# A cross network on one Trainium2 core: TensorE's warm-up cut into 41 products of 128 columns

## The chip, the core and the metric

The kernel runs on one core of one Trainium2 chip. A core has a matrix engine (TensorE; the profile writes PE for its products and PEld for its weight loads), three engines for elementwise work (VectorE or DVE, ScalarE or ACT, GpSimd or POOL), a queue engine (SyncE or SP), and 16 transfer engines that carry all DMA traffic. The working memory has 128 partitions; TensorE writes its results to a second memory, PSUM, of eight banks of 512 fp32 columns per partition. Every engine works through its own list of instructions in order and waits on semaphores that other engines or finished transfers raise.

The metric is device time in microseconds (us), from the first to the last thing that the program does on the chip. It is given as the median of several runs of the same program.

## The reference

The computation is the cross network of a recommender model, "DCN v2", over 4096 rows of 416 features with six layers, in bf16:

```python
B, F, D, L = 4096, 26, 16, 6
Din = min(F * D, 1024)          # 416
x0 = normal(B, Din) * 0.05
ws = normal(L, Din, Din) * 0.05
bs = normal(L, Din) * 0.05

def reference(x0, ws, bs):
    x = x0
    for l in range(ws.shape[0]):
        x = x0 * (x @ ws[l] + bs[l]) + x
    return x
```

Each layer is a product of the current 4096 x 416 matrix with a 416 x 416 matrix, a bias, an elementwise product with the first input, and a sum.

## The kernel before

**Tiling.** The features are the contraction of each layer, so the kernel keeps the activations transposed: features on the partitions, rows of the batch along the free dimension. 416 features are three full blocks of 128 (`XM`, written 0 to 2 as `m` or `k`) and a rest of 32 (`XR`). The batch is cut into two halves `s` of 2048 rows, and each half into four groups `g` of 512 columns. The rests of four groups are stacked on the 128 partitions of `XR`, so that one elementwise instruction handles four groups of 32.

**Inputs.** `x0` comes in twice. Its first 384 features are brought in by eight transposing transfers (`load_x0t`, line 77, all on SP's queue), each for one group of 512 rows, straight into `XM[0]`. The last 32 features (`xrem`) come as they lie in memory, with 64-byte segments (`load_xrem`, line 82): for the first half of the batch in two transfers of 64 partitions each on ScalarE's queue (lines 111 and 314), for the second half in one on SP's queue (line 123). They are turned on VectorE, 32 x 32 at a time (`x0_rem`, lines 160 to 167): a transpose (line 164), copies into `XR[0]` (line 165, one on ScalarE and one on VectorE), and a swapped copy `XRx` (line 167). The first of these two transfers is issued by ScalarE behind its copy of `bsb` (the biases) at line 110, and so after the biases are there; the second is issued behind ScalarE's copy of the first half of `XR`, and so after the first one has landed and been turned. Weights come over ScalarE's queue for layer 0 and over SP's for the others.

**Order of work.** The program runs under a manual schedule: the order of the instructions in the source is the order on each engine. TensorE's list is: the warm-up; layer 0 of the first half of the batch (`first_layer(0)`); layer 0 of the second half; layers 1 to 4 (`for l in range(1, LL)`), in which both halves and the three blocks `m` follow each other; and the last layer, which is computed with the batch rows on the partitions so that the result can be written without a transpose.

**The start of layer 0.** In `first_layer(0)` TensorE first makes six blocks of three untiled products each of 512 columns (line 252, 18 products: three blocks `m` for each of the first two groups), then six products with the 32 remaining features (line 260), for which `XR[0]`'s first 64 partitions must be ready. Then come 72 column-tiled products for the other two groups (line 252 again, four of them side by side in the array), 12 products for the rest of the output (`mm_rem`, line 227), and then six products of line 260 that need the second 64 partitions of `XR[0]`.

**The warm-up.** Before TensorE has any data it multiplies a constant tile `warm` (128 partitions x 512 columns of 0.5) by itself into PSUM bank 0; the result is never read, since the first real product into that bank starts a new sum. VectorE fills `warm` in two instructions, columns 0 to 127 first (line 87), then 128 to 511 (line 88). The function is `pe_filler(n, cols)` at line 151; each call makes n products with the same 128 x 128 weights and cols moving columns. Lines 155 to 157 call it.

**Instructions.** Each product in the source is two instructions on TensorE, a weight load and the product itself. The loops are unrolled in Python, so that the whole program is one straight list for each engine; the transfers of kind "instruction" in the profile bring these lists in.

Of the kernel before, what the change touches and what calls it, by code (L numbers as in the profile page):

```python
# [16 lines left out]
def kernel(  # L17
# [10 lines left out]
    P = 128  # L28
# [5 lines left out]
    CW = 512  # L34
# [116 lines left out]
    def pe_filler(n, cols):  # L151
        for i in range(n):
            nc.tensor.matmul(PS[:, 0, 0:cols], lhsT=warm[:, 0:P], rhs=warm[:, 0:cols], start=True, stop=True, skip_group_check=True)  # L153

    pe_filler(3, P)
    pe_filler(9, CW)
    pe_filler(1, 2 * P)


    def x0_rem(s, p0, p1, parts):  # L160
# [346 lines left out]
```

## Time and profile before

| | |
|---|---|
| time, median of three runs | 129.51 us (129.34 to 129.51) |
| the profiled execution's own time | 130.67 us |
| its span, first to last instruction | 128.9 us |
| TensorE busy | 122.7 us, 1839 products |
| VectorE busy | 104.9 us |
| ScalarE busy | 85.9 us |
| GpSimd busy | 7.8 us |
| warm-up (line 153) | 13 products, 1.04 to 5.65 us |
| first real product (line 252) | 5.79 us |

How to read the profile: all times count from the start of the span. A row of the timeline has the start in us, the duration in us, the engine, the source line, the operation, what it writes `<-` what it reads, the shape, and `x` the number of instructions that were merged into the row; in brackets stands how long the engine had been idle before it and what ended that. A row of the chain has start, duration, engine or transfer, tile and line; the chain is followed back from the last instruction through whatever released each step. "issue" is time in which an engine waited for nothing that the profile shows. A row of the windows view has a stretch of the span, its length, the busy time of each engine asked for with the number of instructions in it, the granted TensorE clock (1.00 is full), the mean busy share of the 16 transfer engines and GB/s. A row of the transfer view has either a queue (q1 is SP's, q10 ScalarE's, q8 and q14 instruction lists) with its packets, megabytes and the time of its packets as a share of 16 engines over the window, or an issue with its count, size and median time from issue to landing.

[...]

### The profile page before, as it was taken

What the parts mean: (1) busy time and instruction counts of PE and PEld (TensorE: products, weight loads), DVE (VectorE), ACT (ScalarE), POOL (GpSimd) and SP (SyncE); (2) the same over time, 40 slices, a digit from 0 to 9 for tenths busy, and PEclk for the clock granted to TensorE, in tenths of its full rate; (3) what the DMA queues carried; (4) which work ended last, traced back from release to release, by engine and by line L of the source; (5) the groups of instructions that cost most, each with busy time, mean ns of one, the idle gap of its engine ahead of it and who ended that gap; (6) DMA issues with size and microseconds to landing.
All of it is one profiled execution on the core that took longest, in us unless ns stands there. A gap on an engine that the chain in (4) does not pass through costs nothing.

```text
span 128.9 us, 4251 instructions
## 1 busy us (share of the span) xinstructions
PE 122.7 (95%) x1839; PEld 55.5 (43%) x1839; DVE 104.9 (81%) x192; ACT 85.9 (67%) x99; POOL 7.8 (6%) x27
## 2 busy tenths in 40 slices
PE   6999799999999999999999999999999999999960
PEld 3344344444444434444444444444444444554430
DVE  3347399649598989898989898989899999998991
ACT  2657194795875775975775975678486686766860
POOL 4270000120000000000000000000005000000000
PEclk9999999999999999999999999999999999999999
DMA  3999989999991000000000000000398999986463
GB/s 87 264 199 163 196 148 242 221 299 343 335 334 51 8 0 5 0 5 0 5 0 0 5 0 5 0 5 0 65 138 162 120 245 218 225 264 223 149 225 104
DMA packets 41935, 16.31 MB, mean 127 GB/s; under 512 B 30838, under 2 KB 41916, under 8 KB 41916
## 3 DMA queue, kind: packets, MB, share of 16 engines
q1 hardware_dynamic: 39344, 15.53, 54.7%
q10 hardware_dynamic: 2572, 0.51, 2.4%
q8 instruction: 14, 0.23, 0.8%
q14 instruction: 5, 0.04, 0.1%
HBM read 6.07 MB, written 3.41 MB: 74 GB/s over the span
## 4 chain that ended last, share of the span: by engine, by line
PE 79%; DMA 10%; DVE 6%; issue 1%; ACT 1%; POOL 0%; DVEq 0%; POOLq 0%
PE PS L208 49%; PE PS L348 9%; DMA xrem<-in_x_dram 7%; PE PS L252 6%; PE PS L214 5%; PE PS L227 5%; DMA bsb<-in_bs_dram 3%; PE PS L220 2%; DVE o L445 2%; DVE t L442 1%; PE PS L260 1%; PE PS L357 1%; DVE xrt L164 1%; DVE o L428 1%; DVE t L425 1%; PE PS L361 1%
## 5 line engine op out<-in xcount | busy, mean ns | idle before, releaser
L172 ACT ACTIVATE t<-PS,bM 128x1024 bf16<-128x1024 f32 x56 | 58.1, 1114 | 23.6 <-PE PS L214 22.8
L208 PE MATMUL PS<-XM,WM 128*32 128x512 bf16 x1152 | 65.2, 380 | 0.0
L208 PEld LDWEIGHTS <-WM 128*32 128x32 bf16 x1152 | 29.7, 97 | 33.8 <-issue 5.1
L182 DVE TENSOR_TENSOR t<-t,XM 128x1024 bf16<-128x1024 bf16 x48 | 33.2, 691 | 5.5 <-ACT t L172 5.4
L183 DVE TENSOR_TENSOR XM<-t,XM 128x1024 bf16<-128x1024 bf16 x48 | 33.5, 698 | 2.6
L348 PE MATMUL PS<-WM,XM 128*128 128x416 bf16 x96 | 17.9, 340 | 0.0
L252 PE MATMUL PS<-XM,WM 128*32 128x512 bf16 (+1 forms) x234 | 16.5, 381 | 0.1
L424 ACT CAST t<-PS 128x832 bf16<-128x832 f32 x12 | 10.1, 854 | 4.3 <-PE PS L348 2.9
L348 PEld LDWEIGHTS <-XM 128*128 128x128 bf16 x96 | 8.9, 98 | 8.6 <-issue 2.1
L252 PEld LDWEIGHTS <-WM 128*32 128x32 bf16 (+1 forms) x234 | 7.8, 97 | 8.4 <-issue 1.8
L227 PE MATMUL PS<-XM,WM 128*32 128x512 bf16 x120 | 8.2, 379 | 0.0
L214 PE MATMUL PS<-XR,WR 32*128 32x512 bf16 x96 | 7.5, 379 | 0.0
L428 DVE TENSOR_TENSOR o<-t,XLrows 128x832 bf16<-128x832 bf16 x12 | 7.0, 592 | 0.4
L425 DVE TENSOR_TENSOR t<-t,X0rows 128x832 bf16<-128x832 bf16 x12 | 7.0, 587 | 0.4 <-ACT t L424 0.4
L180 DVE TENSOR_TENSOR XM<-t,XM 128x1024 bf16<-128x1024 bf16 x7 | 4.9, 697 | 2.7 <-ACT t L172 2.7
L196 ACT ACTIVATE t<-PS,bR 128x512 bf16<-128x512 f32 x10 | 6.8, 695 | 0.0
L326 POOL COPY XLrows<-scrR 128x512 bf16<-128x512 bf16 x2 | 1.7, 894 | 70.8 <-DMA scrR<-XR 70.8
L153 PE MATMUL PS<-warm 128*128 128x512 bf16 (+2 forms) x13 | 4.6, 536 | 1.0 <-DVE warm L87 1.0
L164 DVE STREAM_TRANSPOSE xrt<-xrem 64x256 bf16<-64x256 bf16 (+1 forms) x5 | 2.2, 476 | 4.0 <-DMA xrem<-in_x_dram 4.0
L441 ACT CAST t<-PS 128x416 bf16<-128x416 f32 x8 | 4.0, 505 | 1.0 <-PE PS L348 0.8
L189 ACT ACTIVATE t<-PS,bM 128x512 bf16<-128x512 f32 x4 | 2.6, 685 | 3.0 <-PE PS L260 3.0
L227 PEld LDWEIGHTS <-WM 128*32 128x32 bf16 x120 | 3.2, 97 | 3.3
(47 smaller groups left out, 54.9 us busy)
## 6 DMA issues: line engine op xcount, KB each, us to landing
X0rows<-in_x_dram SPq DMA_DIRECT2D x8, 416.0 KB, 7.8
WM<-in_ws_dram SPq DMA_DIRECT2D x5, 312.0 KB, 5.2
out_dram<-o SPq DMA_DIRECT2D x3, 416.0 KB, 4.6
out_dram<-o SPq DMA_DIRECT2D x6, 208.0 KB, 2.1
out_dram<-o SPq DMA_DIRECT2D x8, 104.0 KB, 1.7
WR<-in_ws_dram SPq DMA_DIRECT2D x4, 104.0 KB, 4.9
WM<-in_ws_dram ACTq DMA_DIRECT2D x1, 312.0 KB, 3.4
XM<-in_x_dram SPq DMA_TRANSPOSE x8, 5.4
```

Source lines behind the costliest of these rows:

```text
L172: nc.scalar.activation(t[:], pt.rearrange("p a b -> p (a b)"), ACT.Identity, bias=bM[:, m, l:l + 1], scale=1.0)
L182: nc.vector.tensor_tensor(out=t, in0=t, in1=x0c, op=ALU.mult)
L183: nc.vector.tensor_tensor(out=nxt[:, m, c0:c0 + 2 * CW], in0=t, in1=cur[:, m, c0:c0 + 2 * CW], op=ALU.add)
L196: nc.scalar.activation(tr[:, 0:CW], pr, ACT.Identity, bias=bR[:, l:l + 1], scale=1.0)
L208: nc.tensor.matmul(pts[g // 2][32 * q:32 * q + 32, g % 2, :], lhsT=WM[:, l, k, 128 * m + 32 * q:128 * m + 32 * q + 32], rhs=cur[:, k, c0:c ...
L214: nc.tensor.matmul(pts[g // 2][:, g % 2, :], lhsT=WR[32 * g:32 * g + 32, l, 128 * m:128 * m + 128], rhs=curR[32 * g:32 * g + 32, CW * s:CW ...
L227: nc.tensor.matmul(pr[32 * g:32 * g + 32, :], lhsT=WM[:, l, k, NK * P:D], rhs=cur[:, k, c0:c0 + CW], start=(first and k == 0), stop=((not ...
L252: nc.tensor.matmul(pt[q0:q1, gl, :], lhsT=WM[:, 0, k, 128 * m + q0:128 * m + q1], rhs=cur[:, k, c0:c0 + CW], start=(first and k == 0), sto ...
L348: nc.tensor.matmul(py[g // 2][:, g % 2, 0:D], lhsT=xL[:, k, q_cols(q, g)], rhs=WM[:, LL, k, :], start=(first and k == 0), stop=((not first ...
L424: nc.scalar.copy(tv, py[h][:, :, 0:D])
L425: nc.vector.tensor_tensor(out=tv, in0=tv, in1=X0rows[:, b0:b0 + 5:4, :], op=ALU.mult)
L428: nc.vector.tensor_tensor(out=o, in0=tv, in1=XLrows[:, b0:b0 + 5:4, :], op=ALU.add)
```

## The change

The three calls of the warm-up become one. Before, it is three products of 128 columns, nine of 512 and one of 256; after, 41 of 128. The weights, the tile `warm`, the PSUM bank and everything before and behind stay as they are.

```diff
@@ -152,9 +152,7 @@
         for i in range(n):
             nc.tensor.matmul(PS[:, 0, 0:cols], lhsT=warm[:, 0:P], rhs=warm[:, 0:cols], start=True, stop=True, skip_group_check=True)
 
-    pe_filler(3, P)
-    pe_filler(9, CW)
-    pe_filler(1, 2 * P)
+    pe_filler(41, P)
 
 
     def x0_rem(s, p0, p1, parts):
```

P is 128 and CW is 512. With `pe_filler(41, P)` no product reads columns 128 to 511 of `warm`; VectorE's second fill (line 88) stays in the program. Lines behind the change have numbers smaller by two in the kernel after.

## The prediction

> **What bounds the kernel now.** I read the page's busy table first, then the chain of work that ended last in order of time between 4 and 17 us, then the timeline of TensorE for the same stretch.
>
> ```profile
> PE 122.7 (95%) x1839; PEld 55.5 (43%) x1839; DVE 104.9 (81%) x192; ACT 85.9 (67%) x99; POOL 7.8 (6%) x27
> ```
> ```profile
> 4.70 3.97 DMA xrem<-in_x_dram
> 9.16 5.58 DMA xrem<-in_x_dram
> 14.76 0.78 DVE xrt L164 x2
> 15.57 0.38 DVE XR L165
> 16.00 0.78 PE PS L260 x6
> ```
> ```profile
> 1.04 4.61 PE L153 MATMUL PS<-warm 128*128 128x128 bf16 x13 [1.04 <-DVE warm L87]
> 5.79 4.31 PE L252 MATMUL PS<-XM,WM 128*128 128x512 bf16 x18
> 10.03 0.60 PE L260 MATMUL PS<-XR,WR 32*128 32x512 bf16 x4
> 10.30 0.39 PE L260 MATMUL PS<-XRx,WR 32*128 32x512 bf16 x2
> 10.62 4.07 PE L252 MATMUL PS<-XM,WM 128*32 128x512 bf16 x72
> 14.51 0.82 PE L227 MATMUL PS<-XM,WM 128*32 128x512 bf16 x12
> 16.00 0.60 PE L260 MATMUL PS<-XR,WR 32*128 32x512 bf16 x4 [0.66 <-DVE XR L165]
> ```
>
> TensorE is busy 95% of the span, but up to 16.0 us it does not set the end. There the chain runs through transfers: the first half of `xrem`, then the second half (issued 9.16, landed 5.58 later at 14.74), VectorE's transpose and copy, and then the product of line 260. TensorE has run dry 0.66 us before that product, and the warm-up is on no piece of this chain. The list of TensorE's waits has, beside the start, one row:
>
> ```profile
> PE PS L260 <- DVE XR L165: 0.7, 1, 0.7
> ```
>
> After 16.0 us it waits for no engine and no transfer. So the end moves by what moves the product at 16.00 us, and 0.66 us of lateness on TensorE before it is free.
>
> **The change part by part.** Columns first: 3 x 128 + 9 x 512 + 256 = 5248 and 41 x 128 = 5248. The same number streams; 13 products become 41, each with its weight load, so TensorE gets 28 products and 28 loads more (56 instructions). No transfer, wait or other engine's instruction moves in the code.
>
> *Duration of the warm-up.* Weight loads on TensorE by time (start, duration):
>
> ```profile
> 1.12 0.26 PEld L153 LDWEIGHTS <-warm 128*128 128x128 bf16 x2
> 1.23 0.15 PEld L153 LDWEIGHTS <-warm 128*128 128x128 bf16 x1
> 4.81 0.15 PEld L153 LDWEIGHTS <-warm 128*128 128x128 bf16 x1 [0.28 <-issue]
> 5.23 0.42 PE L153 MATMUL PS<-warm 128*128 128x256 bf16 x1
> 5.79 0.10 PEld L252 LDWEIGHTS <-WM 128*128 128x128 bf16 x1 [0.41 <-issue]
> 6.17 0.15 PEld L252 LDWEIGHTS <-WM 128*128 128x128 bf16 x1 [0.28 <-issue]
> 6.48 3.12 PEld L252 LDWEIGHTS <-WM 128*128 128x128 bf16 x15 [0.16 <-issue]
> ```
>
> The last 512-column piece starts with the load at 4.81, 5.23 - 4.81 = 0.42 us before the next piece; the 128-column ones are at the start 1.23 - 1.12 = 0.11 us apart: the load of the next piece runs while this one streams, in both shapes. 41 pieces at 0.11 us start last at 1.04 + 40 x 0.11 = 5.4 us, against 5.23 us for the 256-column piece now, whose columns end half a 0.42 later, about 5.45 us; the new last piece's end 0.11 later, about 5.5 us. The first real product starts at 5.79 us either way, because its transposed block of `x0`, issued at 0.71 us, lands at 5.7:
>
> ```profile
> XM<-in_x_dram SPq DMA_TRANSPOSE x1, 5.0
> ```
>
> The cover is those 0.3 us, and behind them the 0.66 us. The 512-column pieces also waited for VectorE's second fill of `warm`; the new ones need the first fill alone, worth under 0.1 us, which nobody sees. Cost: 0. Without the cover it would be what the pitch exceeds 0.11 us by, times 41.
>
> *Pace of TensorE.* The granted clock reads 1.00 in every window quoted below (third column from the end), yet the starts above say otherwise: 0.4 us per 512 columns until about 6.2 us, then 3.12 us for 15 pieces (0.21 each). The pace doubles after some 5 us of products. The new warm-up streams the same columns over the same time, so I take the doubling as unmoved: 0. The ends: 0.2 us earlier per real product for the two slow ones (a gain that the wait at 16.0 us swallows), and the late opening priced under the rivals.
>
> *Instruction fetch: the moved step.* 56 more instructions ahead of everything else shift all later fetches of TensorE's instruction stream. The page's queue list, windows of the transfer view (one line each, windows 15.3 to 15.5, 22.5 to 22.7, 38.3 to 38.4, 49.9 to 50.0, 57.0 to 57.1 us; the share is of 16 engines over the window), and the products started by then:
>
> ```profile
> q8 instruction: 14, 0.23, 0.8%
> ```
> ```profile
> q8 instruction: 1, 0.02, 30.4%
> q8 instruction: 1, 0.02, 40.8%
> q8 instruction: 1, 0.02, 68.3%
> q8 instruction: 1, 0.02, 86.4%
> q8 instruction: 1, 0.02, 83.2%
> ```
> ```profile
> 0.00:15.40 15.40, 14.16 (x121) 1.00 1.04 188
> 0.00:22.60 22.60, 20.76 (x235) 1.00 1.00 186
> 0.00:38.40 38.40, 36.56 (x519) 1.00 1.05 236
> 0.00:49.90 49.90, 48.06 (x723) 1.00 0.82 187
> 0.00:57.00 57.00, 55.16 (x851) 1.00 0.72 164
> ```
>
> Each fetch is one packet of 0.23 MB / 14 = 16 KB; the one at 15.3 to 15.5 us took 0.304 x 16 x 0.2 = 0.97 us of one transfer engine. In the quiet stretch they come 851 - 723 = 128 products apart (with their loads 256 instructions), so they follow the count: 723 = 5 x 128 + 83, hence the first belongs to product 83. Product 83 is number 83 - 13 - 18 - 6 = 46 of the 72 that start at 10.62 us; four take 0.215 us (15 untiled ones 3.12 us; four tiled share a pass), so it starts at 10.62 + 46/4 x 0.215 = 13.1 us. The fetch came at 15.4, 2.3 us later, while transfers were busy; the second came 235 - 128 - 83 = 24 products late (1.3 us at 0.054), the fourth 519 - 3 x 128 - 83 = 52 (2.8 us). So under load the lag is 1.3 to 2.8 us. After the change the 83rd product is what is now the 55th, 18th of the 72: 10.62 + 18/4 x 0.215 = 11.6 us, and the fetch comes at 12.9 to 14.4 us instead of 15.4. What else moves then, in the same view for 11.5 to 13.77 us:
>
> ```profile
> q10 hardware_dynamic: 1040, 0.07, 40.2%
> ```
>
> Queue 10 is ScalarE's, and its only transfer then is the second half of `xrem` (0.07 MB): all of it lies between 11.5 and 13.77 us, and it is the one on the critical chain. A 16 KB packet put in front of an engine's share holds that share up. What that does shows on the transfers that the present fetch hits, issued 10.63 and 13.68 us; median times to landing, with neighbours:
>
> ```profile
> 10.63 3.00 SPq L77 DMA_TRANSPOSE XM<-in_x_dram  x1
> 13.68 0.65 SPq L82 DMA_DIRECT2D xrem<-in_x_dram  x1
> ```
> ```profile
> XM<-in_x_dram SPq DMA_TRANSPOSE x1, 6.8
> XM<-in_x_dram SPq DMA_TRANSPOSE x1, 5.9
> xrem<-in_x_dram SPq DMA_DIRECT2D x1, 128.0 KB, 4.3
> ```
>
> The transpose under way at 15.4 us took 6.8 us where the next took 5.9: +0.9. The `xrem` load of the other half took 4.3 where the first one took 3.97 in the chain: +0.3. So a hit costs 0.3 to 0.97 us (the packet itself); I take 0.7, nearer the transpose, since the second half of `xrem` crawls among transposes. The wait at 16.0 us gives no cover here: it is this landing that it waits for. A miss costs nothing, and the present hit costs nothing either, so no gain from its going: the product at 16.93 us starts without a wait.
>
> [...]
>
> *Later fetches* move 28 products (28 x 0.054 = 1.5 us) earlier too; what they slow then is loaded ahead of its use, since TensorE waits for nothing after 16 us. 0, or a part of 0.97 us where a load has less lead than the rows show.
>
> **Sum.** The profiled execution has a span of 128.9 us and took 130.67 us; the three timed runs have a median of 129.51. Span 128.9 + 0.7 = 129.6; on the median 129.51 + 0.7 = 130.2 us.
>
> **The rivals.**
> *The fetch misses* (before the load's packets, after 13.77, or behind its share of that engine). For it: with the same lag of 2.3 us it comes at 11.6 + 2.3 = 13.9 us, just past; 12.9 to 13.77 is only 58% of the interval. Time: 129.5, within 0.25. This is also the outcome if the change only cuts the same columns otherwise.
>
> *The pace doubles later or the pieces run slower.* If 128-column pieces came at the 0.15 us of their weight load, the warm-up would end at 1.04 + 41 x 0.15 = 7.2 us, 1.4 us behind 5.79; less the 0.66 free, less 0.4 us for two or three real products that then run at full pace: 0.3 us, 129.9. It costs from a pitch of 0.132 us on ((5.79 + 0.66 - 1.04)/41). Against it: the loads at 1.12 and 1.23. If narrow pieces did not count as work, the doubling would come only 5 us after 5.79, near 11: 5 us at half pace lose 2.5 us, less 0.26 lost now and 0.66 free: +1.6, 131.1. [...] Against it: the array streams as continuously as now.
>
> *Faster: the second half of `xrem` lands earlier.* The profile is one execution; in the timed ones, without a profiler, the fetch may fall elsewhere and hit that load already now, and the shift may free it. Price: as much as the hit, 0.7, but at most the 0.66 us for which TensorE waits: 128.85. It decides wherever the load lands early, since VectorE then stands ready:
>
> ```profile
> 14.76 0.77 DVE L164 STREAM_TRANSPOSE xrt<-xrem 64x256 bf16<-64x256 bf16 x2 [2.13 <-DMA xrem<-in_x_dram]
> ```
>
> Against it: in the trace shown the fetch starts 1.5 us behind the load's last packet.
>
> **How the numbers follow.** Fetch hits: 0.43. Misses: 0.30. Pace or pitch: 0.10. Freed: 0.17. Likeliest 130.2, its own range 129.8 to 130.5. The 8-in-10 range takes the freed case nearly whole and the pace cases to the middle: 128.9 to 130.9. Within 0.2% (0.26 us, about what a measurement tells from no change): 0.30; slower 0.53; faster 0.17.
>
> **What would show it.** After: 41 starts 0.107 to 0.11 apart; first real product within 0.1 of 5.79; q8's first packet between 12.9 and 14.4 us; `xrem`'s second landing at 15.4 rather than 14.74; the wait before line 260 near 1.4 us rather than 0.66; everything behind shifted alike. Wrong if that landing stays (129.5), if the real products still come 0.4 us apart after 7 us, or if TensorE waits in a place that has no wait now.

## The result, and the profile after

The changed kernel takes 130.84 us (median of five runs, 130.61 to 130.98); the kernel before, run beside it, 129.51 (129.34 to 130.2). The ratio is 1.0091, with a 95% interval of 1.0068 to 1.0115: slower by 1.3 us. A second set of runs gave 1.0081 (1.0054 to 1.0108).

TensorE by time in the kernel after (start, duration, line; its line 250 is line 252 of the kernel before, 258 is 260, 225 is 227):

```profile
1.04 4.56 PE L153 MATMUL PS<-warm 128*128 128x128 bf16 x41 [1.04 <-DVE warm L87]
5.66 4.07 PE L250 MATMUL PS<-XM,WM 128*128 128x512 bf16 x18
14.12 0.83 PE L225 MATMUL PS<-XM,WM 128*32 128x512 bf16 x12
15.65 4.35 PE L250 MATMUL PS<-XM,WM 128*32 128x512 bf16 x72
20.22 0.60 PE L258 MATMUL PS<-XR,WR 32*128 32x512 bf16 x6 [0.23 <-DVE XR L163]
21.64 4.10 PE L250 MATMUL PS<-XM,WM 128*32 128x512 bf16 x72 [0.70 <-DMA XM<-in_x_dram]
```

and its weight loads:

```profile
1.03 4.29 PEld L153 LDWEIGHTS <-warm 128*128 128x128 bf16 x41 [1.03 <-DVE warm L87]
5.28 0.15 PEld L250 LDWEIGHTS <-WM 128*128 128x128 bf16 x1
```

The warm-up itself costs nothing: the 41 loads take 5.28 - 1.03 = 4.25 us to the next one, 0.104 apart on average, and the first real product starts at 5.66 us, against 5.79 and 5.58 in the two profiles of the kernel before. The time is lost later. At 21.64 us TensorE has waited 0.70 us for a block of `x0` of the second half, a wait that neither profile of the kernel before shows, and the chain behind the last instruction goes through that transfer:

```profile
14.17 7.43 DMA XM<-in_x_dram
21.60 0.04 issue
21.64 4.10 PE PS L250 x72
```

This block, the third of the second half of the batch, was issued at 14.17 us and took 7.43 us to land; all eight transposing transfers of this profile have a median of 5.2. What held it up is seen in the windows of the transfers (stretch, its length, TensorE busy, products, granted clock, transfer share, GB/s):

```profile
13.60:14.20 0.60, 0.60 (x20) 1.00 1.38 246
14.20:14.30 0.10, 0.10 (x8) 1.00 20.47 97
14.30:15.60 1.30, 1.30 (x25) 1.00 0.11 6
19.70:20.30 0.60, 0.38 (x12) 1.00 2.40 157
20.70:21.40 0.70, 0.24 (x4) 1.00 0.21 10
21.60:22.20 0.60, 0.56 (x12) 1.00 1.27 289
```

Twice, for 1.3 us from 14.3 and for 0.7 us from 20.7, hardly any data moves: 6 and 10 GB/s, against 246 and 289 in the stretches ahead and behind. The share counts a packet's whole duration where the packet starts. The second row has 20.47 of 16 engines' time over 0.1 us in 38 packets, which is 20.47 x 1.6 / 38 = 0.9 us a packet; in the 0.1 us from 13.6 it is 1.215 x 1.6 / 108 = 0.018. So packets are held here, about until the stop is over. The fourth row, with 2.40 at only 157 GB/s, has held packets too. Each stop follows a fetch of TensorE's instructions. The transfer view of 13.6 to 13.7 us, and of 19.65 to 19.75 us, has one line for queue 8 each:

```profile
q8 instruction: 1, 0.02, 79.2%
q8 instruction: 1, 0.02, 60.5%
```

From their share of 16 engines over 0.1 us, the two packets took 0.792 x 1.6 = 1.27 and 0.605 x 1.6 = 0.97 us. In the profile shown before, the fetches were at 15.4 and 22.6 us, and at 14.7 and 22.1 us in the second one below. So 28 products more have moved the first by 1.1 to 1.8 us and the second by 2.4 to 2.9 us.

That profile of the kernel before is not a typical one. The profiled execution took 130.67 us where the median is 129.51, and the 0.66 us wait for the second 64 partitions of the first half's `xrem`, on which the prediction leans, belongs to it. Such executions are not rare: of the 23 of the kernel before that ran beside the first experiments, 16 took 129.27 to 130.25 us and seven 130.72 to 131.07. A second profile of the unchanged kernel (first experiment, 129.74 us, span 127.9) has TensorE there as follows:

```profile
15.20 0.39 PE L260 MATMUL PS<-XR,WR 32*128 32x512 bf16 x2
15.96 4.06 PE L252 MATMUL PS<-XM,WM 128*32 128x512 bf16 x72
19.95 0.60 PE L260 MATMUL PS<-XR,WR 32*128 32x512 bf16 x6
20.49 4.10 PE L252 MATMUL PS<-XM,WM 128*32 128x512 bf16 x72
```

No wait stands in these rows. Set against them, the kernel after is 0.31 us ahead at the second half's first block (15.65 against 15.96), 0.27 behind at the rest products (20.22 against 19.95) and 1.15 behind at the next block (21.64 against 20.49). The spans differ by 129.1 - 127.9 = 1.2 us. So the loss arises between 15.7 and 21.6 us, and nothing more is lost behind it. The lateness at the rest products comes from `xrem` of the second half, which the first stop holds up (5.3 us to landing, in the first profile before 4.3). It adds nothing at the end, because the block's landing at 21.60 us comes later still. A second profile of the kernel after (last experiment) shows this: its rest products are early and do not wait, and the block starts at 21.62 us all the same.

```profile
19.61 0.60 PE L258 MATMUL PS<-XR,WR 32*128 32x512 bf16 x6
```

In the second profile of the kernel before the same block was issued at 14.03 us, with this time to landing:

```profile
XM<-in_x_dram SPq DMA_TRANSPOSE x1, 5.8
```

It landed at 14.03 + 5.8 = 19.8 us, some 0.6 us ahead of its use at 20.49. This is its lead, and 7.43 us instead of 5.8 use it up.

### The profile page after: what moved, and what is told of

The parts are those of the page before. It is cut to its first block, busy times and chain, and to the rows that moved or that the text cites. A ratio compares the mean times of both kernels' runs of the same rounds, so it can differ in the third digit from the quotient of the medians.

```text
span 129.1 us, 4307 instructions
## 1 busy us (share of the span) xinstructions
PE 122.6 (95%) x1867; PEld 58.1 (45%) x1867; DVE 105.0 (81%) x192; ACT 86.1 (67%) x99; POOL 7.9 (6%) x27
## 4 chain that ended last, share of the span: by engine, by line
PE 75%; SPq 10%; DMA 6%; DVE 5%; issue 1%; ACT 1%; DVEq 0%
PE PS L206 49%; SPq L77 10%; PE PS L346 9%; DMA XM<-in_x_dram 6%; PE PS L212 5%; PE PS L225 5%; PE PS L250 3%; DVE o L443 2%; PE PS L218 2%; DVE t L440 1%; PE PS L355 1%; DVE o L426 1%; DVE t L423 1%; PE PS L359 1%; ACT t L422 1%
## 5 line engine op out<-in xcount | busy, mean ns | idle before, releaser
L170 ACT ACTIVATE t<-PS,bM 128x1024 bf16<-128x1024 f32 x56 | 58.3, 1115 | 24.4 <-PE PS L212 22.8
L250 PE MATMUL PS<-XM,WM 128*32 128x512 bf16 (+1 forms) x234 | 16.5, 380 | 0.9 <-DMA XM<-in_x_dram 0.7
L153 PE MATMUL PS<-warm 128*128 128x128 bf16 x41 | 4.6, 313 | 1.0 <-DVE warm L87 1.0
L153 PEld LDWEIGHTS <-warm 128*128 128x128 bf16 x41 | 4.3, 150 | 1.0 <-DVE warm L87 1.0
```

The costliest lines, as they stand in the source:

```text
L170: nc.scalar.activation(t[:], pt.rearrange("p a b -> p (a b)"), ACT.Identity, bias=bM[:, m, l:l + 1], scale=1.0)
L250: nc.tensor.matmul(pt[q0:q1, gl, :], lhsT=WM[:, 0, k, 128 * m + q0:128 * m + q1], rhs=cur[:, k, c0:c0 + CW], start=(first and k == 0), sto ...
```

## The experiments

The theories, as the expectations name them. **F**: the place of TensorE's instruction fetches among the input transfers decides. Later it is split: **F1**, the first fetch costs the time; **F2**, the second one does, because it moved from a time when all transposed blocks had landed into the last two of them. **W**: the narrow pieces themselves cost it, by their pace, their loads or a later full pace.

**The kernel before again.** No edit.

> The kernel before once more, unchanged, for a second profile of it. Theory F (the place of TensorE's instruction fetch among the transfers of the input decides): time within 0.2% of the kernel before (ratio 0.998 to 1.002); first fetch between 14.5 and 16 us, no hold-up of all transfers between 13.5 and 15.5 us, no wait of TensorE for a transposed block of x0 in the second half's layer 0. Since the profile shown before the change ended 1.2 us later than the median of its own runs, this one should have a span near 127.7 us and not show the 1 us wait ahead of the second half of xrem. Theory W (the narrow pieces themselves are slow or open the clock later): the same time, no statement on transfers.

Ratio 1.0007 (0.9974 to 1.0039). The rows of TensorE are above; the windows of its transfers:

```profile
14.70:16.00 1.30, 1.30 (x26) 1.00 0.84 88
14.80:15.20 0.40, 0.40 (x12) 1.00 0.20 19
16.10:16.30 0.20, 0.20 (x12) 1.00 1.06 96
16.30:17.00 0.70, 0.70 (x20) 1.00 0.15 9
20.50:21.20 0.70, 0.70 (x20) 1.00 1.25 261
22.10:22.70 0.60, 0.60 (x18) 1.00 1.13 214
22.70:23.40 0.70, 0.70 (x20) 1.00 1.08 187
```

Queue 8 has its packets at 14.7 and 22.1 us here. Behind the first, transfers slow to 88 GB/s, with 19 GB/s in the 0.4 us from 14.8 and 9 GB/s in the 0.7 us from 16.3. So a low rate alone does not mark a stop: in the 0.2 us ahead of 16.3 the share is 1.06 and not 20.47, so no packets are held, and TensorE waits for no block of the second half. (A stretch of 12 GB/s from 16.5 to 17.2 us is in the second profile of the kernel after as well, with the first fetch at 13.4 us, so it need not come from the fetch.) Behind the second, only plain loads of weights are under way, and they go on at 214 and 187 GB/s: a fetch does not stop everything always. The time and the missing wait are as F expected; that nothing would be held up from 13.5 to 15.5 us holds but for the 0.4 us. W said nothing on it.

**Wide warm-up, 27 products more elsewhere.** The 18 untiled products that open layer 0 become 9 untiled and 36 column-tiled ones:

```diff
-            tiled = s == 1 or h == 1
+            tiled = s == 1 or h == 1 or gl == 0
```

> The wide warm-up of the kernel before (13 products), but nine of the 18 untiled products that open layer 0 are cut into four column tiles each, as the next 72 are: 27 products and 27 weight loads more ahead of the first fetch, the same passes of the array. Theory F: the first fetch comes about 1.5 us earlier than in the kernel before, near 13.7 us, transfers stop behind it, and the time is that of the narrow warm-up: ratio 1.006 to 1.012 to the kernel before. Theory W: the warm-up is as before, so 0.998 to 1.002.

Ratio 1.0113 (1.0071 to 1.0155), with the warm-up untouched. One row of TensorE, and one of the windows:

```profile
23.25 2.77 PE L252 MATMUL PS<-XM,WM 128*32 128x512 bf16 x48 [0.75 <-DMA XM<-in_x_dram]
```
```profile
20.80:22.20 1.40, 1.40 (x32) 1.00 0.05 5
```

Transfers stop for 1.4 us behind the second fetch (20.5 us), and TensorE waits 0.75 us for a transposed block, the last one. (In this profile TensorE is 0.49 us later than in the second profile of the kernel before already at the second half's first block, 16.45 against 15.96, so not the whole ratio need come from the stop.) The first fetch came at 14.7 us, not at 13.7 as expected, with no more behind it than in the kernel before; the expectation that the first fetch does the harm is not borne out here, which is what split F into F1 and F2.

**Narrow warm-up, 27 products fewer elsewhere.** In the kernel after, nine groups of four column tiles become nine untiled products, ahead of the first fetch:

```diff
-            tiled = s == 1 or h == 1
+            tiled = s == 1 or (h == 1 and gl == 1)
```

> The narrow warm-up (41 products of 128 columns), but nine groups of four column tiles of layer 0's next block are done as one untiled product each: 27 products and loads fewer, so that from product 77 on the count is that of the kernel before, plus one. Theory F: first fetch back at 15 to 15.5 us, time back to that of the kernel before: ratio 0.998 to 1.003. Theory W: still 1.006 to 1.012.

Ratio 0.9967 (0.9926 to 1.0009), a little under what F expected: the whole loss is gone, with all 41 narrow pieces in place. The fetches are at 15.0 and 22.4 us. (The profile is of the longest of its ten executions, 131.03 us, with a wait of 1.24 us at 11.15 us for the first 64 partitions of `xrem`. Behind the first fetch the rate falls to 24 GB/s from 15.4 to 16.0 us; TensorE waits for no block of `x0`.) W falls: with the narrow warm-up alone the ratio was 1.0091.

**21 pieces.**

```diff
-    pe_filler(3, P)
-    pe_filler(9, CW)
-    pe_filler(1, 2 * P)
+    pe_filler(1, P)
+    pe_filler(20, 2 * P)
```

> The same 5248 columns as one product of 128 and 20 of 256: 21 products, 8 more than before instead of 28 more. Theory F: the fetch moves by 8 products, 0.4 us, to about 14.7 to 15 us; the cost is that of where it then falls, between nothing and the whole 0.9%: ratio 1.000 to 1.009, and whatever it is, it goes with a stop of the transfers behind the fetch and a TensorE wait for a block of x0. Theory W: pieces of 256 columns are nearly wide, 1.000 to 1.003, with no such wait.

Ratio 1.006 (1.0028 to 1.0091), between the two kernels. Its executions spread from 129.87 to 131.19 us, and the one with the profile is among the fastest (129.90): its second fetch falls at 20.6 us, on the edge, no stop follows and TensorE has no wait for a block. So the size agrees with F, which allowed anything up to 0.9%, but the stop that it foretold with the loss was not seen: none of the slower executions has a profile, and the kernel before spreads as far (129.27 to 131.07). What its loss comes from is not shown.

**Narrow warm-up, only the second fetch put back.** In the kernel after, nine groups of the second half's first block are done untiled. They lie behind the first fetch and ahead of the second:

```diff
-            tiled = s == 1 or h == 1
+            tiled = (s == 1 or h == 1) and not (s == 1 and h == 0 and (m, gl) in ((0, 0), (1, 0), (1, 1)))
```

> The narrow warm-up (41 products), and nine groups of four column tiles at the start of the second half's layer 0 done as one untiled product each: 27 products fewer, but only behind the first fetch (product 83) and ahead of the second (product 211). Theory F1 (the first fetch, moved into 13 to 14.5 us, costs the 1%): first fetch still early, time 1.006 to 1.012 of the kernel before. Theory F2 (the second fetch costs it, moved from 22 us, where the transposed blocks of x0 have all landed, to 19.7 to 20.5 us, where the last two are under way and all transfers stop for over 1 us): first fetch early, second back at 21.5 us or later, last transposed block landed by 21.5, time 0.997 to 1.003. Theory W (the narrow pieces themselves): 1.006 to 1.012.

Ratio 0.9995 (0.9959 to 1.0032). Windows of the transfers:

```profile
14.10:15.50 1.40, 1.40 (x29) 1.00 0.11 7
20.50:21.40 0.90, 0.90 (x18) 1.00 1.24 281
```

and two rows of TensorE, then the time to landing of the third block of the second half, issued at 13.84 us:

```profile
20.53 2.13 PE L250 MATMUL PS<-XM,WM 128*32 128x512 bf16 x36
22.85 2.13 PE L250 MATMUL PS<-XM,WM 128*32 128x512 bf16 x36 [0.20 <-DVE XM L188]
```
```profile
XM<-in_x_dram SPq DMA_TRANSPOSE x1, 6.4
```

The first fetch is still early (13.6 us) and stops the transfers as in the kernel after, for 1.4 us. The second is back at 22.4 us; where the kernel after had 10 GB/s, 281 GB/s move here. The third block lands at 13.84 + 6.4 = 20.2 us, so the first stop takes some of its lead and not all, and the products at 20.53 do not wait. (The last block lands at 21.7 us, 0.2 later than F2 expected, and is not waited for either.) The time is that of the kernel before within the interval: F2. The first stop is not quite free in this profile: `xrem` of the second half lands late, and 0.20 us of waiting for VectorE comes of it. Its times point the same way, though its mean does not: none of the ten executions is under 129.74 us, where 14 of the 29 of the kernel before beside them are, and none is over 130.44. The interval allows up to 0.3% for the first stop, and cannot tell it from nothing.

**41 pieces, most columns in wide ones.** No product of a layer is touched:

```diff
-    pe_filler(3, P)
-    pe_filler(9, CW)
-    pe_filler(1, 2 * P)
+    def pe_tiny(n):
+        for i in range(n):
+            nc.tensor.matmul(PS[0:32, 0, 0:32], lhsT=warm[:, 0:32], rhs=warm[:, 0:32], start=True, stop=True, tile_position=(0, 0), skip_group_check=True)
+
+    pe_tiny(29)
+    pe_filler(4, P)
+    pe_filler(7, CW)
+    pe_filler(1, 2 * P)
```

> No product of the layers is touched. The warm-up is 29 products of 32 columns with 32-column weights, then 4 of 128, 7 of 512 and one of 256: 41 products, 5280 columns, of which over three quarters stream in the wide pieces. Theories F1 and F2: as the narrow warm-up, 1.006 to 1.012, with the second fetch between 19.5 and 21 us. Theory W: as the wide one, 0.997 to 1.003. If the tiny products come slower than 0.05 us apart, up to 0.8 us of lateness at the first real product is added, which both theories would see by 10 us.

Ratio 1.0076 (1.0039 to 1.0114). TensorE, then three of its windows:

```profile
1.03 0.95 PE L157 MATMUL PS<-warm 128*32 128x32 bf16 x29 [1.03 <-DVE warm L87]
1.92 3.81 PE L153 MATMUL PS<-warm 128*128 128x128 bf16 x12
5.71 4.53 PE L257 MATMUL PS<-XM,WM 128*128 128x512 bf16 x18
21.45 4.10 PE L257 MATMUL PS<-XM,WM 128*32 128x512 bf16 x72 [0.67 <-DMA XM<-in_x_dram]
```
```profile
15.80:16.30 0.50, 0.50 (x11) 1.00 0.11 8
19.90:20.40 0.50, 0.50 (x16) 1.00 2.60 73
20.50:21.20 0.70, 0.27 (x8) 1.00 0.14 11
```

The tiny pieces are over by 1.92 us, the first real product starts at 5.71, as early as ever, and yet the loss is there, at the same block and behind the same stop (second fetch 19.3 us, a little ahead of the stretch expected). A short stop, 8 GB/s for 0.5 us, also follows the first fetch, at 14.5 us. It is the 28 products in the instruction stream that cost, and not the width at which most columns of the warm-up stream.

**Wide warm-up, 27 products fewer.** The edit of the narrow one above, on the kernel before.

> The wide warm-up of the kernel before, with nine groups of four column tiles in the second block of layer 0 as one untiled product each: 27 products fewer than before, same passes. F1 and F2: both fetches come about 1.5 us later than before, the second near 23.5 to 24 us, farther from the transposed blocks: no loss, and the executions of the kernel before that take 130.7 to 131.1 us should be rarer: ratio 0.993 to 1.001. It is also the control for the untiled products: if they cost by themselves, it shows here as over 1.002.

Ratio 0.9992 (0.9958 to 1.0026). The fetches are at 15.2 and 22.8 us, 0.4 and 0.7 us later than in the second profile of the kernel before, and not the 1.5 us expected. So no gain shows from the little that they moved, and the untiled products cost nothing that can be told from noise. Of its 12 runs, one took 130.87 us and the others 129.3 to 130.31.

**A whole block more.** 141 pieces are 128 more than before, the products between two fetches in the first profile of the kernel before (851 - 723), so that the boundaries behind them should fall where they did:

```diff
+    pe_filler(3, P)
+    pe_tiny(136)
+    pe_filler(2, P)
```

> The warm-up is 3 products of 128 columns, 136 of 32 with 32-column weights, and 2 of 128: 141 products, 4992 columns, ending near 5.8 us at 0.031 us for a tiny one. That is 128 products more than in the kernel before, one whole instruction block. Theory F2 (it is where the block boundaries fall, not how many pieces the warm-up has): an extra fetch near 5 to 7 us, and all others where the kernel before has them, at 14.5 to 15.5 and 22 to 23 us, no TensorE wait for the last transposed blocks; ratio 0.997 to 1.004 unless the extra fetch holds up the first inputs. Theory W (more and narrower pieces cost): at least the 1.006 to 1.012 of the narrow warm-up.

Ratio 1.0097 (1.0069 to 1.0126), so it does not speak against W by its time. The trace says where it comes from. TensorE and a window:

```profile
5.62 2.16 PE L256 MATMUL PS<-XM,WM 128*128 128x512 bf16 x9
9.11 2.10 PE L256 MATMUL PS<-XM,WM 128*128 128x512 bf16 x9 [1.33 <-DMA XM<-in_x_dram]
```
```profile
7.20:7.80 0.60, 0.58 (x3) 1.00 0.27 7
```

The extra fetch, at 6.4 us, stops the transfers from 7.2 to 7.8 us, at 7 GB/s, and TensorE waits 1.33 us for the second block of `x0`: the exception that the expectation made. The last blocks are not waited for. The other fetches came only roughly where expected, at 15.8 and 24.8 us, since TensorE itself was late by then. It is a third place at which a fetch among the input's transfers costs about 1 us.

**The kernel after again.** No edit.

> The changed kernel once more, for a second profile and more executions beside tiny141 on one chip. F2: ratio 1.006 to 1.012, second fetch between 19.3 and 20.6 us, a stop of all transfers of 0.6 to 1.5 us behind it, and 0.6 to 0.9 us of TensorE waiting for one of the last two transposed blocks near 21.5 us. W: the same ratio, no statement on transfers.

Ratio 1.0081 (1.0054 to 1.0108). TensorE and a window:

```profile
21.62 4.12 PE L250 MATMUL PS<-XM,WM 128*32 128x512 bf16 x72 [1.35 <-DMA XM<-in_x_dram]
```
```profile
20.10:21.40 1.30, 0.17 (x4) 1.00 0.18 6
```

The same block, 1.35 us of waiting where 0.6 to 0.9 was expected, and a stop of 1.3 us behind a second fetch at 18.9 us, a little ahead of the stretch expected. (The wait is longer than in the first profile because the rest products ahead of it are earlier; the block starts at the same time, 21.62 against 21.64 us.)

No version tried beats the kernel before: the two with a second fetch later than 22 us and nothing else lost lie at 0.9967 and 0.9992, both with 1 inside their intervals.

What stays open: why the fetch of one 16 KB packet stops the other transfers. Stops were seen behind fetches at 6.4, 13.4, 13.6, 14.5 and 18.9 to 20.5 us. They were not seen, or only weakly, behind those at 14.7 to 15.8 us, nor behind one at 20.6 us, nor among plain loads from 22 us on. So the stops came while the input's transfers were under way, and none while plain loads of weights were alone (214 and 187 GB/s), but not behind every fetch among the input's transfers: behind the one at 14.5 us 8 GB/s moved from 15.8 to 16.3 us, with packets held in the 1.1 us from 14.5 us (a share of 1.52 at 88 GB/s), and behind the one at 14.7 us in the second profile of the kernel before 88 GB/s over 1.3 us at a share of 0.84. The transposes alone are not the mark either: in the 0.1 us of the fetch at 6.4 us, `xrem`'s queue 10 has 75.8% of 16 engines' time and queue 1 with the transposes 31.5%. Whether it is the kind of transfer, or the order in which the queues are served, was not tried.

## Why the prediction was right, and where not

It forecast slower, 130.2 us in a range of 128.9 to 130.9, and 130.84 was measured, just inside the upper end. The direction came from the right cause, the 56 instructions that shift TensorE's instruction fetches, but not by the path forecast. The fetch that it priced, the first, hit another transfer than it said and costs at most 0.3% alone; the fetch that it put at nothing, the second, costs the time. The 0.7 us forecast is half of the 1.33 measured. That 130.84 lies in the range is in part luck: the case in which the fetch hits had 129.8 to 130.5 of its own, and the rest up to 130.9 was there for a slower pace, which did not come. One of its own signs of being wrong did come: TensorE waits in a place that had no wait.

- *Duration of the warm-up*: right. Pieces 0.104 us apart, a little closer than the 0.107 to 0.11 forecast, the first real product at 5.66 us.
- *Pace of TensorE*: right in that it costs nothing. The 18 products from 5.66 us take 4.07 us, and the row behind them starts at 9.66 us, so they start (9.66 - 5.66) / 18 = 0.22 us apart: the full pace is there from the start, and no part of the loss lies ahead of 15.6 us. (The 18 take 4.31 and 4.04 us in the two profiles of the kernel before, so the moment at which the pace doubles differs between executions of one kernel.) The rivals on pace and pitch fall, and with them W.
- *The fetch moves to 12.9 to 14.4 us*: right, it came between 13.6 and 13.7 us, counted out as one fetch per 128 products (851 - 723).
- *It hits the second half of `xrem`* (the second 64 partitions for the batch's first half): wrong. That transfer was through by then: VectorE starts on it at 13.24 us, and the products that need it (14.89 us) do not wait. The wait for it in the profile shown was that of the longer execution profiled, as the second profile shows, so neither "0.66 us of lateness on TensorE before it is free" nor "it is this landing that it waits for" held for the kernel as it usually runs. The mismatch of 130.67 against a median of 129.51 stood in the text and was used only to shift the sum; it was the sign that the chain shown was not the usual one.
- *A hit costs one engine's share, 0.3 to 0.97 us*: mis-sized, and wrong in kind. Nearly all traffic stops, for 0.5 to 1.4 us, as the windows at 5 to 11 GB/s show. What the +0.9 of the late transpose came from was not tried; in the second profile of the kernel before, where the first fetch comes as that block is under way too, the same block took 6.1 us.
- *Later fetches: 0*: the step that failed. "TensorE waits for nothing after 16 us" was true of the fetches as they lay, with the second one at 22.1 or 22.6 us, behind the last transposed block (landed at about 21.4 and 22.0 us). It moved farther than the 1.5 us forecast, to 19.7 us, and so lies among the last two blocks. The first of these has a lead of only some 0.6 us, and takes 1.6 us longer to land: putting that one fetch back returns the time to 0.9995, with the first one left early. The sentence allowed "a part of 0.97 us where a load has less lead than the rows show" and gave it no chance.
- *The rivals that the fetch misses* and *faster*: for the first fetch, "misses" is what happened, since it came after the load's packets, and its 129.5 us is near the outcome of that fetch alone (0.9995). The second rival had no part.

## What to carry to other kernels

Instructions were transfers too here, one packet of 16 KB for every 128 products: count the instructions ahead of the first critical loads, find the boundaries in the transfer view, and for an edit that adds or removes instructions shift *every* boundary, not only the first, against the landings that have little lead. A fill-in with equal work but more instructions need not be neutral: 5248 columns in 41 products instead of 13 took 1.0091 of the time. And when the profiled execution is slower than the median of its own runs, take a second profile before a wait in it is called the bound.

## What the hardware showed that I had not expected

A single 16 KB instruction packet can be followed by a stop of nearly all traffic of the core: 6 GB/s for 1.3 us from 14.3 us in the kernel after, though it costs little there, 5 GB/s for 1.4 us from 20.8 us with the tiled opening, 7 GB/s for 0.6 us from 7.2 us with 141 pieces. The stops began 0.3 us (fetch at 20.5 us, tiled opening) to 1.3 us (fetch at 14.5 us, tiny pieces) behind the packet's start and outlasted the packet, which took 0.93 us (58.3% of 16 engines over 0.1 us, 141 pieces) to 1.75 us (109.2%, the second profile of the kernel after). And pieces of 32 columns with 32-column weights run 0.031 us apart at the start of the warm-up (29 in 1.92 - 1.03 us), against 0.104 for those of 128 with 128, so filling TensorE's time with small pieces takes many more instructions.
